# Rotation tables from tables held in pairs, ahead of slab 1's statistics, and slab 0's second token half in quarters

## The chip, the cores and the metric

The kernel runs on one NeuronCore of a Trainium2 chip. The core has five engines that run side by side, each with an instruction queue of its own that is worked off in order: TensorE (PE, matrix products), VectorE (DVE), ScalarE (ACT), GpSimd (POOL) and SyncE (SP, which here only issues DMAs). They meet through semaphores. TensorE writes to PSUM, which this kernel uses as eight banks of 128 x 512 fp32. The metric is device time in microseconds for one execution; all times below are microseconds unless marked otherwise.

## The reference

The input `x` has 2048 tokens of 512 features. What is computed, cut to what matters:

```python
xn = (x - mean(x)) / sqrt(var(x) + 1e-5)                 # per token
dt = exp(log_dt); Lam_bar = exp(dt * (Lambda_re + 1j * Lambda_im))
B_bar = ((Lam_bar - 1) / Lam)[:, None] * Bmat            # 512 complex states
Bu = einsum("bld,pd->blp", xn, B_bar)
for t in range(2048):
    h = Lam_bar * h + Bu[t]
s = 2 * einsum("blp,dp->bld", h, Cmat).real + xn * Dskip
g = silu((gelu(xn @ w_gate) * (xn @ w_up)) @ w_down)     # 512 -> 1376 -> 512
out = x + s * g
```

## The kernel before

**Tiling.** The tokens go in four slabs (`NS`) of 512 (`TS`), each in four blocks of 128 tokens. For a slab, `ffn` (L459) runs eleven steps `j` over the 1376 hidden features: gate and up products into two PSUM banks (`gu_mm`, L236), GELU and copy on ScalarE, their product on VectorE in pairs of steps (`at`). `u_pair` (L372) makes the products with B in two halves, `chain` rotates them by a complex table, runs the scans on VectorE and rotates back into `hst`. `down` (L482) multiplies `at` with `w_down` into `f_ps`, 11 products for each block. `y_mm` (L502) and `epi` (L514) of a slab run inside the `ffn` steps of the next one, at the steps that `Y_AT` names; `y_seed` (L497) fills their PSUM bank first, on ScalarE.

**Rotation.** The complex recurrence becomes a real one by rotating with cos and sin of the angle times the token number. The tables `cos_b` and `sin_b` hold 512 columns for each of four groups of states. They come from small ones: with token = 32a + b, cos and sin of 32a (`NA` = 16 values) and of b (`NB` = 32 values) are taken with ScalarE's Sin (`sh`, `ch`, 49 columns), and VectorE makes the large table with four products and two sums (L614, L624 to L628). The angles come from GpSimd, L206 to L214, out of `pf` (L205). GpSimd copies the values of 32a out to full width, `sa` and `ca` (L284, L285), so that the products read them densely.

**Order.** Every engine's order is the order of the program's text (`manual_schedule`). For VectorE a small planner writes it: `later` puts work in a list with a due time and a cost; `dve` gives out an operation that is due at a time, and ahead of it `drain` pops from the front of the list what fits by the clock `clk["dve"]`; `flush` pops up to a named item. The clock of TensorE advances by 0.2157 a product.

**Head of slab 0.** Ten filler products (`dummies`) surround the transpose of the small parameters. Blocks 0 and 1 are loaded first, their statistics (`bn`, `bn_end`), square root and reciprocal (`rstd0`) and norm (`norm0`) follow, TensorE transposes (`t_xn0`) and VectorE and ScalarE copy to `xnT`. `gu_mm` then runs the first 256 tokens of steps 0 to 3 (`SPLIT` = 4, `early`) while blocks 2 and 3 are prepared; one PSUM bank holds the transposes of both. `ffn` adds the second 256 tokens.

**Slab 1's input.** VectorE takes its statistics (L612), GpSimd its `rs`, VectorE norms it with `norm1` (L619), and SyncE issues four DMA transposes to `xnT` (`xn_out`, L585). These are issued in steps 3 to 6 of slab 0. At step 6 SyncE is also given four DMA transposes of C's real part, the two loads of `wd`, and four transposes of C's imaginary part (L651 to L658), in this order:

```python
                if 3 <= j < 3 + M:
                    flush(("xn", j - 3))
                    xn_out(1, j - 3, xs1[j - 3])
                if j == 2 + M:
                    load_c(0)
```

Ahead of them its queue holds the loads of tokens, gate and up weights and the transposes of B. `wd` is first read by slab 0's `down`, behind both `u_pair`s of slab 1, which read slab 1's `xnT`.

## Time and profile before

| | |
|---|---|
| median of 13 runs | 185.78 (185.56 to 186.16) |
| profiled execution, its own time | 186.08 |
| its span on the core | 183.5 |
| busy in the span: TensorE, VectorE, ScalarE, GpSimd | 176.1, 160.5, 116.9, 27.2 |
| slab 0's first product of step 4 starts | 15.88 |
| slab 1's `u_ps` products, slab 0's `f_ps` products start | 34.88, 41.78 |
| largest gap of TensorE behind the head | 1.17, at 101.86 |

The span runs from the first to the last instruction of the core; what the device time has beyond it, 2.6 here, lies around it. Starts are counted from the span's start. A row of the timeline gives start, length, engine, line of the kernel, operation, output and inputs, shapes, count, and in brackets how long the engine stood idle before it and what it waited for. Rows with DMA and an engine's name with q (SPq) are issues of transfers, whose length is that of the issue, not of the transfer. Lengths of products on TensorE overlap their neighbours.

### The profile page before, as it was taken

How to read it: one execution, taken by the hardware profiler on the slowest of the kernel's cores; microseconds unless marked ns; L12 is line 12 of the kernel's file. 1: busy time of each engine (PE TensorE's matmuls, PEld its weight loads, DVE VectorE, ACT ScalarE, POOL GpSimd, SP SyncE). 2: the span in 40 equal slices, each digit the busy share in tenths (PEclk: the TensorE clock that was granted, in tenths of full speed). 3: DMA queues.
4: the chain of work that ended last, by engine and by line, in shares of the span. 5: the costliest groups of instructions: out<-in, count | busy, mean ns of one | idle time of the engine just before them, and what ended most of it. 6: DMA issues, size and time to landing. Idle time of an engine off the chain costs nothing.

```text
span 183.5 us, 2441 instructions
## 1 busy us (share of the span) xinstructions
PE 176.1 (96%) x855; PEld 83.8 (46%) x855; DVE 160.5 (87%) x251; ACT 116.9 (64%) x207; POOL 27.2 (15%) x50
## 2 busy tenths in 40 slices
PE   6989999999999999999999799999999999999992
PEld 2666444544444444444444344444444444444451
DVE  3589999899999899899958999999999999996063
ACT  3299666668789974475499775667529445574510
POOL 3879917000700000000004000000000000000000
PEclk9999999999999999999999999999999999999999
DMA  5999594690001400101300023300000000000012
GB/s 159 299 350 158 101 238 108 186 278 0 0 0 29 84 5 29 50 7 30 113 4 0 0 59 84 88 5 0 0 0 0 0 30 32 29 29 0 0 47 68
DMA packets 25643, 12.37 MB, mean 67 GB/s; under 512 B 15808, under 2 KB 25632, under 8 KB 25632
## 3 DMA queue, kind: packets, MB, share of 16 engines
q1 hardware_dynamic: 25456, 12.16, 27.1%
q8 instruction: 6, 0.10, 0.2%
q10 hardware_dynamic: 176, 0.07, 0.1%
q14 instruction: 5, 0.04, 0.1%
HBM read 6.46 MB, written 2.10 MB: 47 GB/s over the span
## 4 chain that ended last, share of the span: by engine, by line
PE 73%; DVE 9%; ACT 8%; DMA 3%; POOL 2%; issue 2%; ACTq 1%; SPq 0%; DVEq 0%; POOLq 0%
PE up_ps L243 17%; PE g_ps L243 17%; PE f_ps L487 14%; PE y_ps L507 13%; PE u_ps L382 11%; DVE Ft L429 3%; ACT junk L552 2%; DMA x_tok<-in_A_x_dram 2%; DVE yg L520 2%; DVE pp L399 1%; DMA pv<-in_A_Dskip_dram 1%; ACT gt L471 1%; ACT ub L472 1%; ACT g L492 1%; DVE ot L521 1%
## 5 line engine op out<-in xcount | busy, mean ns | idle before, releaser
L243 PE MATMUL up_ps<-xnT,wu 128*128 128x512 bf16 (+2 forms) x192 | 45.7, 361 | 0.8 <-ACT xnT L201 0.8
L243 PE MATMUL g_ps<-xnT,wg 128*128 128x512 bf16 (+3 forms) x196 | 45.9, 357 | 0.3 <-DVE xnT L203 0.3
L487 PE MATMUL f_ps<-wd,at 128*128 128x512 bf16 (+1 forms) x176 | 38.9, 379 | 0.1
L471 ACT ACTIVATE gt<-g_ps 128x512 bf16<-128x512 f32 (+1 forms) x44 | 26.7, 608 | 17.0 <-PE g_ps L243 16.6
L472 ACT ACTIVATE ub<-up_ps 128x512 bf16<-128x512 f32 (+1 forms) x44 | 26.9, 612 | 6.7 <-PE up_ps L243 6.3
L429 DVE TENSOR_TENSOR_SCAN Ft<-rho,it,Wt 128x512 bf16<-128x512 f32 x24 | 29.3, 1267 | 0.0
L507 PE MATMUL y_ps<-C,hst 128*128 128x512 bf16 x120 | 28.0, 379 | 1.2 <-ACT y_ps L499 1.2
L382 PE MATMUL u_ps<-xnT,BT 128*128 128x512 bf16 x128 | 28.4, 379 | 0.0
L243 PEld LDWEIGHTS <-wu 128*128 128x128 bf16 (+1 forms) x192 | 19.2, 100 | 19.8 <-issue 1.0
L243 PEld LDWEIGHTS <-wg 128*128 128x128 bf16 (+1 forms) x196 | 19.3, 100 | 19.2 <-issue 0.4
L487 PEld LDWEIGHTS <-at 128*128 128x128 bf16 (+1 forms) x176 | 17.1, 98 | 21.1 <-DVE at L478 0.5
L387 ACT ACTIVATE U<-u_ps 128x512 bf16<-128x512 f32 x32 | 19.0, 597 | 9.8 <-PE u_ps L382 9.7
L382 PEld LDWEIGHTS <-BT 128*128 128x128 bf16 x128 | 12.5, 98 | 15.1
L492 ACT ACTIVATE g<-f_ps 128x512 f32<-128x512 f32 x16 | 9.5, 593 | 15.2 <-PE f_ps L487 15.2
L507 PEld LDWEIGHTS <-hst 128*128 128x128 bf16 x120 | 11.7, 98 | 15.5 <-issue 1.5
L520 DVE TENSOR_TENSOR yg<-y_ps,g 128x512 bf16<-128x512 f32 x15 | 10.2, 683 | 9.1 <-PE y_ps L507 9.0
L480 DVE TENSOR_TENSOR at<-gt,ub 128x1024 bf16<-128x1024 bf16 x20 | 13.6, 682 | 1.6 <-ACT ub L472 1.5
L403 DVE TENSOR_TENSOR hst<-pp,qq 128x1024 bf16<-128x1024 bf16 x16 | 10.4, 688 | 0.3
L403 DVE TENSOR_TENSOR Wt<-pp,qq 128x1024 bf16<-128x1024 bf16 x16 | 10.4, 686 | 0.2
L399 DVE TENSOR_TENSOR pp<-U,cos_b 128x2048 bf16<-128x2048 bf16 x8 | 9.7, 1219 | 0.0
L399 DVE TENSOR_TENSOR pp<-Ft,cos_b 128x2048 bf16<-128x2048 bf16 x8 | 9.7, 1217 | 0.0
L399 DVE TENSOR_TENSOR qq<-U,sin_b 128x2048 bf16<-128x2048 bf16 x8 | 9.7, 1216 | 0.0
(108 smaller groups left out, 153.6 us busy)
## 6 DMA issues: line engine op xcount, KB each, us to landing
out_dram<-ot SPq DMA_DIRECT2D x15, 128.0 KB, 1.7
x_tok<-in_A_x_dram SPq DMA_DIRECT2D x3, 512.0 KB, 6.8
wd<-in_B_w_down_dram SPq DMA_DIRECT2D x1, 1280.0 KB
wg<-in_B_w_gate_dram SPq DMA_DIRECT2D x2, 256.0 KB, 4.2
wu<-in_B_w_up_dram SPq DMA_DIRECT2D x2, 256.0 KB
wg<-in_B_w_gate_dram SPq DMA_DIRECT2D x1, 512.0 KB, 6.1
wu<-in_B_w_up_dram SPq DMA_DIRECT2D x1, 512.0 KB
wg<-in_B_w_gate_dram SPq DMA_DIRECT2D x1, 352.0 KB
```

The lines of the kernel that those rows point to most:

```text
L243: nc.tensor.matmul(ps[:fs, a:b], lhsT=w[:, kt, fsl], rhs=xnT[:, kt, s * TS + a : s * TS + b], start=(kt == 0), stop=(kt == KT - 1),)
L382: nc.tensor.matmul(u_ps[:, :], lhsT=BT[:, ri, kt, pt * P : (pt + 1) * P], rhs=xnT[:, kt, cols], start=(kt == 0), stop=(kt == KT - 1),)
L387: ACT(out=U[:, ri, q, :], in_=u_ps[:, :], func=AF.Copy)
L399: TT(out=box[key][:], in0=src()[:], in1=tab[:, hs, :].unsqueeze(1).to_broadcast(W), op=ALU.mult)
L403: return lambda: TT(out=dst()[i], in0=box["pp"][:, i, :, :], in1=box["qq"][:, 1 - i, :, :], op=op)
L429: nc.vector.tensor_tensor_scan(out=box["F"][:, ri, q, :], data0=rho[:, pt : pt + 1].to_broadcast([P, TS]), data1=box["W"][:, ri, q, :], in ...
L471: ACT(out=gt[:fs, i, :], in_=g_ps[:fs, :], func=AF.Gelu_apprx_tanh)
L472: ACT(out=ub[:fs, i, :], in_=u_ps[:fs, :], func=AF.Copy)
L480: dve(now() + lag, 0.63, lambda: TT(out=at[:, j - 1 : j + 1, :], in0=gt[:], in1=ub[:], op=ALU.mult))
L487: nc.tensor.matmul(f_ps[:, :], lhsT=at[:fs, k, m0 : m0 + P], rhs=wd[:fs, k, :], start=(k == 0), stop=(k == NFT - 1))
L507: nc.tensor.matmul(y_ps[:, :], lhsT=hst[:, j // NPT, j % NPT, m0 : m0 + P], rhs=C2[:, j // NPT, j % NPT, :], start=False, stop=(j == 2 * N ...
L520: TT(out=yg[:], in0=y_ps[:, :], in1=g2[:], op=ALU.mult)
```

## The change

Small tables in pairs: GpSimd no longer copies 32a's cos and sin to full width. It writes each value twice, side by side (`s2a`, `c2a`, 128 columns), and the four products read them with a five-dimensional pattern whose innermost dimension is the pair.

Order: the table's six operations stand at the front of VectorE's list. Slab 1's statistics follow them, popped at step 5, its `rs` behind them, the norms and the four transposes at step 6, and C and `wd` are issued at step 7. The products of slab 0's tokens with `Dskip` (`skip`) come behind the statistics.

Head: statistics, square root and reciprocal of blocks 0 and 1 come ahead of `pf` in the text; eight filler products and one instead of six and four; `Abs` moves behind the first Sin. `SPLIT` is 3; blocks 2 and 3 are transposed into a bank each, both copied by VectorE, and steps 0 (gate, up) and 1 (gate) take the second token half in quarters of 128, block 2 first. Step 3 runs whole.

Slab 2: slab 1's output products move from steps 3 to 6 to steps 4 to 7. The planner's starting clocks change with all this.

```diff
-    dummies(6)
+    dummies(8)
     pt_ps = psum.tile([P, 16], BF16, name="pt_ps", tag="ps")
     nc.tensor.transpose(pt_ps[:, :], pv[:, :], ident[0:16, 0:16])
-    dummies(4)
+    dummies(1)
...
+    for m in range(2):
+        bn(0, m)
+    bn_end(0, 0)
+    bn_end(0, 1)
+    rstd0(0, 2)
     ACT(out=pf[:], in_=pt_ps[:, :], func=AF.Copy)
...
-    for m in range(2):
-        bn(0, m)
-    bn_end(0, 0)
-    bn_end(0, 1)
-    rstd0(0, 2)
     xs = [norm0(0), norm0(1)]
...
-    ACT(out=kr[:], in_=ang[:], func=AF.Abs)
     rstd0(2, 4)
     ACT(out=tiny[:], in_=halfpi[:], func=AF.Sin)
     xs += [norm0(2), norm0(3)]
-    SPLIT = 4
+    SPLIT = 3
...
-    for up in range(2):
-        early[2, up] = gu_mm(0, 2, up, 0, TS // 2)
-    tp2 = psum.tile([P, 2, KT, P], BF16, name="tp", tag="ps")
-    for i in range(2):
-        t_xn0(2 + i, xs[2 + i], tp2[:, i, :, :])
-    for up in range(2):
-        early[3, up] = gu_mm(0, 3, up, 0, TS // 2)
-    xnT_out(nc.vector, 2, tp2[:, 0, :, :])
+    early[2, 0] = gu_mm(0, 2, 0, 0, TS // 2)
+    tps.append(t_xn0(2, xs[2]))
+    early[2, 1] = gu_mm(0, 2, 1, 0, TS // 2)
+    tps.append(t_xn0(3, xs[3]))
+    for m in range(2, M):
+        xnT_out(nc.vector, m, tps[m])
+    for m in range(2, M):
+        for j, up in ((0, 0), (0, 1), (1, 0)):
+            gu_mm(0, j, up, m * P, (m + 1) * P, early[j, up])
     ACT(out=sh[:], in_=ang[:], func=AF.Sin, scale=TWO_PI)
+    ACT(out=kr[:], in_=ang[:], func=AF.Abs)
     ACT(out=ch[:], in_=kr[:], func=AF.Sin, scale=-TWO_PI, bias=halfpi[:])
-    xnT_out(nc.scalar, 3, tp2[:, 1, :, :])
...
-    nc.gpsimd.tensor_copy(out=v4(sa[:]), in_=sh[:, :, NB : NB + NA].unsqueeze(3).to_broadcast(W4))
-    nc.gpsimd.tensor_copy(out=v4(ca[:]), in_=ch[:, :, NB : NB + NA].unsqueeze(3).to_broadcast(W4))
-    cB = ch[:, :, 0:NB].unsqueeze(2).to_broadcast(W4)
-    sB = sh[:, :, 0:NB].unsqueeze(2).to_broadcast(W4)
+    c2a, s2a = (consts.tile([P, NPT, NA, 2], BF16, name=n) for n in ("c2a", "s2a"))
+    for o, i in ((s2a, sh), (c2a, ch)):
+        nc.gpsimd.tensor_copy(out=o[:], in_=i[:, :, NB : NB + NA].unsqueeze(3).to_broadcast([P, NPT, NA, 2]))
+    sa, ca = (o[:].unsqueeze(3).to_broadcast(W5) for o in (s2a, c2a))
+
+    def of_b(t):
+        return t[:, :, 0:NB].rearrange("p k (b c) -> p k b c", c=2).unsqueeze(2).to_broadcast(W5)
+
+    cB, sB = of_b(ch), of_b(sh)
...
-    Y_AT = {1: (8, 9, 10, 11), 2: (3, 4, 5, 6), 3: (2, 4, 6, 8)}
+    Y_AT = {1: (8, 9, 10, 11), 2: (4, 5, 6, 7), 3: (2, 4, 6, 8)}
...
         if s == 0 and j < SPLIT:
-            g_ps, u_ps = (gu_mm(s, j, up, TS // 2, TS, early[j, up]) for up in range(2))
+            g_ps, u_ps = early[j, 0], early[j, 1]
+            for up in range(2):
+                if j == 2 or (j == 1 and up):
+                    gu_mm(s, j, up, TS // 2, TS, early[j, up])
...
-    clk["pe"] = 6.8
-    clk["dve"] = 13.1
-    clk["act"] = 12.4
+    clk["pe"] = 6.9
+    clk["dve"] = 10.6
+    clk["act"] = 12.6
...
-    ln_vector(1)
-    ln_vector_small(1)
-    later(13.0, 1.25, lambda: TT(out=v4(t2_[:]), in0=v4(sa[:]), in1=sB, op=ALU.mult))
+    later(10.5, 1.25, lambda: TT(out=v5(t2_[:]), in0=sa, in1=sB, op=ALU.mult))
+    later(11.2, 1.25, lambda: TT(out=v5(t1_[:]), in0=ca, in1=cB, op=ALU.mult))
+    later(11.2, 1.25, lambda: TT(out=cos_b[:], in0=t1_[:], in1=t2_[:], op=ALU.subtract))
+    later(11.2, 1.25, lambda: TT(out=v5(t1_[:]), in0=sa, in1=cB, op=ALU.mult))
+    later(11.2, 1.25, lambda: TT(out=v5(t2_[:]), in0=ca, in1=sB, op=ALU.mult))
+    later(11.2, 1.25, lambda: TT(out=sin_b[:], in0=t1_[:], in1=t2_[:], op=ALU.add))
+    for m in range(M):
+        later(0.0, 0.72, lambda m=m: (bn(1, m), bn_end(1, m)), "n1")
...
-    for m in range(M):
-        later(15.8, 0.36, lambda m=m: norm1(m), ("xn", m))
...
-                if 3 <= j < 3 + M:
-                    flush(("xn", j - 3))
-                    xn_out(1, j - 3, xs1[j - 3])
-                if j == 2 + M:
+                if j == 5:
+                    flush("n1")
+                    ln_vector_small(1)
+                    rs1_at = clk["dve"] + 2.4
+                if j == 6:
+                    for m in range(M):
+                        dve(max(rs1_at, now() - 0.8), 0.36, lambda m=m: norm1(m), 0.4)
+                        xn_out(1, m, xs1[m])
+                if j == 7:
                     load_c(0)
```

## The prediction

> **What bounds the kernel now.** I read the page's busy line first, then the timeline of TensorE for its gaps, then the queues that feed the first slab: SyncE, VectorE, the DMA packets.

> ```profile
> PE 176.1 (96%) x855; PEld 83.8 (46%) x855; DVE 160.5 (87%) x251; ACT 116.9 (64%) x207; POOL 27.2 (15%) x50
> ```

> TensorE is busy 96%, so the time is its work plus its gaps. Its timeline has few, and these rows carry them:

> ```profile
> 11.96 0.60 PE L243 MATMUL up_ps<-xnT,wu 128*128 128x256 bf16 x4 [0.79 <-ACT xnT L201]
> ...
> 34.88 7.07 PE L382 MATMUL u_ps<-xnT,BT 128*128 128x512 bf16 x32
> 41.78 9.68 PE L487 MATMUL f_ps<-wd,at 128*128 128x512 bf16 x44
> ...
> 101.86 1.89 PE L507 MATMUL y_ps<-C,hst 128*128 128x512 bf16 x8 [1.17 <-ACT y_ps L499]
> ```

> From 11.96 to the end only one gap is shown, 1.17 at 101.86. So a gain at the head counts in full unless a feeder becomes late, and a feeder that becomes late by more than its slack costs in full. The SyncE queue is the feeder that the change moves:

> ```profile
> 21.80 0.50 SPq L98 DMA_DIRECT2D wu<-in_B_w_up_dram  x1
> 22.42 5.13 SPq L587 DMA_TRANSPOSE xnT<-xn  x4
> 27.61 5.22 SPq L106 DMA_TRANSPOSE CT<-in_A_C_re_dram  x4
> 32.88 0.58 SPq L653 DMA_DIRECT2D wd<-in_B_w_down_dram  x1
> 33.50 0.65 SPq L657 DMA_DIRECT2D wd<-in_B_w_down_dram  x1
> ```

> It runs without a pause: the normalised slab 1 has been ready since about 20 (last L171 row of VectorE below), so nothing waits for data. `wd` goes out last, and its second piece lands 6.2 later, at 39.7; TensorE wants `wd` at 41.78.

> ```profile
> wd<-in_B_w_down_dram SPq DMA_DIRECT2D x1, 96.0 KB, 6.2
> ```

> The packets of 38.75 to 39.00 and of the next quarter microsecond show the last of `wd` (its rows are 1 KB; the transposes' packets are under 512 B):

> ```profile
> DMA packets 250, 0.07 MB, mean 275 GB/s; under 512 B 240, under 2 KB 250, under 8 KB 250
> DMA packets 171, 0.04 MB, mean 161 GB/s; under 512 B 171, under 2 KB 171, under 8 KB 171
> ```

> So the big piece of `wd` lands between 38.9 and 39.7; I take 39.4, a slack of 2.4 that no wait row shows. Last, VectorE around the tables:

> ```profile
> 11.11 2.46 DVE L160 BATCH_NORM_STATS2 st<-x_tok 128x6 f32<-128x512 bf16 x4
> 13.77 2.20 DVE L614 TENSOR_TENSOR t__264<-sa,sh 128x2048 bf16<-128x2048 bf16 x1
> ...
> 19.41 0.40 DVE L171 TENSOR_SCALAR xn<-x_tok,mv,rs 128x512 bf16<-128x512 bf16 x1
> ...
> 20.78 1.25 DVE L624 TENSOR_TENSOR t__263<-ca,ch 128x2048 bf16<-128x2048 bf16 x1
> ```

> Slab 1's statistics come first, the five other table operations (1.25 each) last. That is what the change turns round.

> [...] A transpose that waits for its source therefore holds every later DMA of SyncE. The trace agrees: output stores stood 101.3 in all on that queue for VectorE's `ot`, and the load of slab 3's tokens left only behind one of them, at 86.01. [...] the 2.20 product overlaps the wide GpSimd copy (12.97 to 14.86), the others take 1.25. [...] the trace shows full speed behind its 1.17 gap and nothing of longer ones.

> **The change part by part.** *Head.* Moving the square root ahead of `pf` starts it at about 4.36 (statistics end 4.30) instead of 4.58; eight dummies end at about 4.6 (start spacing 0.43), one more at 5.1, so slab 0's transposes start when their weights can load, about 5.55, not 6.08. First product at 6.7 (7.22 before), the second quarter after ACT's copy at 7.3 (about 7.6). Then four halves at 0.435: 9.26 with `[2,g]`. `Abs` no longer stands before the second square root: it starts at 8.1 (9.03), the norms end at 9.35 (10.27). `pf` is 0.3 later, so are GpSimd's angles (9.04), still before `sh` at 9.8. Transposes, `[2,u]`, transposes end at 10.23 (0.27 per four, from eight in 0.54). VectorE copies both blocks, to 10.14 and 10.84. Six quarters at 0.22 to 0.27 run 10.23 to 11.85, the rest of j=1, 2 (3 x 0.435) to 13.15, j=3 whole (1.73) to 14.9. Before, j=4 starts at 15.88. **Gain 1.0** (0.5 to 1.3; the clock of the first products varies). ACT's first GELU moves from 13.51 to about 12.4, so the PSUM banks free in time.

> *Tables.* Two GpSimd copies of 1.89 become 128-element copies (0.2 to 0.5, between the 49- and 196-element rows), hidden beside the slab's head. GpSimd's twelve coefficient operations then run at 11 to 17 instead of 18 to 23.5, ahead of `rs`; those that overlapped table operations before left these at 1.25, so I add nothing. The four products: low bound 1.2 each (as now, and never 2.20)[...]. I take 1.2[...].

> *VectorE's new order.* Following the planner's clocks (start 10.6) through `drain`: t2, t1, cos, t1 | at j1 | t2 | at j3 | sin | at j5 | statistics x4 (flushed at j=5) | z x4 | pp | norm x4. `pp` gets ahead of the norms because 24.31+1.17 is within 25.27+0.4. With durations of the trace: start 10.9; four table operations of about 1.23 to 15.85; at 0.6, t2 1.2, at 0.6, sin 1.2, at 0.6 to 20.05 (all three GELU pairs are ready before); statistics 4 x 0.80 (rows at 42.48 to 45.69) to 23.25; z 4 x 0.335 to 24.6; pp 1.15 to 25.75; first norm done 26.15. GpSimd's `rs` takes 2.2 after the last statistics (45.77 to 47.98 in slab 2), so 25.45: hidden by z and pp.

> *SyncE.* Its first transpose of slab 1 leaves at 26.2 instead of 22.42: **the queue is 3.8 late**, idle since 22.3. Queued behind it: three transposes, four of C (re), `wd`, `wd`'s end, four of C (im). First, xnT: last issue 30.05, landing 2.4 to 3.4 later, 33.5 at most; TensorE wants it at 33.9. It holds, by 0.4. Second, `wd`: 39.4 + 3.8 = 43.2; TensorE, 1.0 early, wants it at 40.8 and **stands 2.4**. Third, C (im): first block about 42.5; ACT wants it at 46.3, after `f_ps`.

> *Sum at `f_ps`.* It starts at 43.2 instead of 41.78: **+1.4**. The head's gain is wholly eaten: once `wd` ends last, only the queue's lateness less the slack counts (3.8 - 2.4). Behind it VectorE, some 2 earlier relative to TensorE than before, only waits longer for ACT's `tA`, and slabs 1 to 3 keep their distances to TensorE. [...] I add nothing for the clock.

> *Slab 2.* The first y product moves behind j=4. ACT does GELU and copy of j=3 (0.97) and one norm (0.71) ahead of the seed, so it ends at 103.4 and not 101.8; TensorE arrives at 102.4 and not 100.7. The gap is 1.05 instead of 1.17: **-0.1**. Bounds: 0 to -0.5 if a norm slips behind.

> Total +1.3: span 184.8, and with the 2.6 around it (186.08 less 183.5) 187.4 for an execution like the profiled one. That one lies 0.3 above the median 185.78, so I name **187.1**.

> **Rivals.** *A, the load is covered after all.* Place: `wd` before the first `f_ps`. Price: the head's 1.0 and slab 2's 0.1 then count, 184.7. It decides if the queue is under 2.4 late (break-even), in full under 1.4, that is with the first norm done by 24.8 or 23.8; or if the transfer lands in less than its 6.2. For it: 6.2 includes a queue behind C's packets till 33.9, and 1.4 MB at the 380 GB/s shown in the middle need only 3.7. Against: the same transposes precede it afterwards, and all but four VectorE durations are read from rows. *B, pairs read slowly.* [...] *C, it cancels*: slack 3 and lateness 3.1 leave +0.1 less 0.1, 185.8. Before, the big piece landing at 38.9 gives 2.9 of slack, so this is near one end of the bounds.

> **How the numbers follow.** My forecast 63%, B 15%, A 15%, C 7%. The forecast's own range is 186.2 to 188.3: slack 1.5 (landing 40.3, if 6.2 counts from the issue's end) to 2.9, queue late 3.3 to 4.4 (start of the tables 10.6 to 11.5). I give 184.9 to 189.6: it leaves out the deeper half of A and the upper half of B and its overshoot. A measurement of this kernel tells about 0.2% (0.37) from no change. Faster, from A: 15%; same, from C: 7%; slower, forecast and B: 78%.

> **What would show it.** Right: SyncE's transposes of xnT at about 26.2, not 22.4; `wd` issued near 36.7; a gap of about 2.4 before L487's first matmul, put down to a DMA of `wd`; j=4 on TensorE near 14.9; table products at 1.2; the gap before slab 2's first y product about 1. Wrong: L487 starting before 41.7[...]; or a gap at `u_ps` of slab 1 that is longer than the one at `f_ps`.

## The result, and the profile after

The kernel after takes **188.75 us** in the median of 11 runs (187.04 to 190.47), beside 185.87 for the kernel before (48 runs). The ratio is 1.0122, 95% interval 1.0099 to 1.0146: slower by about 1.2%. The forecast was 187.1, range 184.9 to 189.6. The ratio is taken without executions more than 1.5% above the fastest, so it lies below the quotient of the medians.

The executions differ, and their mean granted clock of TensorE says how. With the profiled one there are twelve:

| mean granted clock | executions | time | span |
|---|---|---|---|
| 1.0 | 4 | 187.04, 187.10, 187.15, 188.26 | 184.8 to 185.1 |
| 0.990 to 0.991 | 6 | 188.55 to 190.47 | 186.3 to 187.0 |
| 0.982 | 2 | 190.29, 190.61 | 188.0, 188.3 |

The profiled execution is the slowest, 190.61 with a span of 188.3. From the page, the busy line and the clock (40 slices of 4.7 us; each digit is tenths of full speed, 9 for 0.9 and more):

```profile
PE 178.1 (95%) x858; PEld 83.9 (45%) x858; DVE 160.6 (85%) x252; ACT 116.5 (62%) x206; POOL 23.2 (12%) x50
...
PEclk9789999997899999999999999999999999999999
```

TensorE's clock was at half speed twice, from 7.29 to 10.70 and from 44.83 to 48.25, each time for 3.41. The timeline of TensorE shows what this cost:

```profile
7.04 1.93 PE L242 MATMUL g_ps<-xnT,wg 128*128 128x128 bf16 x12 [0.19 <-DVE xnT L203]
8.77 1.91 PE L242 MATMUL up_ps<-xnT,wu 128*128 128x256 bf16 x8
...
16.30 1.03 PE L242 MATMUL g_ps<-xnT,wg 128*128 128x512 bf16 x4
...
35.30 7.07 PE L386 MATMUL u_ps<-xnT,BT 128*128 128x512 bf16 x32
...
45.22 11.15 PE L494 MATMUL f_ps<-wd,at 128*128 128x512 bf16 x44 [2.85 <-DMA wd<-in_B_w_down_dram]
...
108.39 1.89 PE L514 MATMUL y_ps<-C,hst 128*128 128x512 bf16 x8 [1.07 <-ACT y_ps L506]
```

Ahead of `f_ps` TensorE stands 2.85, waiting for a load of `wd`; before, it did not stand there at all. Then the same 44 products take 11.15, where before they took 9.68. In stretches of this execution (start and end, length, busy time and count of TensorE, clock, share and rate in GB/s of the DMA engines):

```profile
40.00:42.00 2.00, 2.00 (x11) 1.00 0.96 309
42.00:44.00 2.00, 0.37 (x2) 1.00 1.14 361
44.00:46.00 2.00, 0.78 (x2) 0.71 1.48 80
46.00:48.00 2.00, 2.00 (x6) 0.50 0.87 169
48.00:50.00 2.00, 2.00 (x10) 0.94 0.00 0
```

The clock drops to half while TensorE stands and comes back a little over 48: in 46 to 48 six products start where eleven did before the stand. SyncE's queue shows why `wd` came late (issues only):

```profile
22.31 0.50 SPq L98 DMA_DIRECT2D wu<-in_B_w_up_dram  x1
27.58 5.12 SPq L594 DMA_TRANSPOSE xnT<-xn  x4
32.75 5.17 SPq L106 DMA_TRANSPOSE CT<-in_A_C_re_dram  x4
37.97 0.58 SPq L662 DMA_DIRECT2D wd<-in_B_w_down_dram  x1
38.60 0.65 SPq L666 DMA_DIRECT2D wd<-in_B_w_down_dram  x1
```

The queue is idle from 22.8 to 27.6, waiting for slab 1's norms, and `wd` leaves at 37.97 where it left at 32.88 before. VectorE's rows ahead of that:

```profile
12.45 1.25 DVE L619 TENSOR_TENSOR t__276<-s2a,sh 128x2048 bf16<-128x2048 bf16 x1
...
26.01 1.22 DVE L403 TENSOR_TENSOR pp<-U,cos_b 128x2048 bf16<-128x2048 bf16 x1
27.15 1.37 DVE L171 TENSOR_SCALAR xn<-x_tok,mv,rs 128x512 bf16<-128x512 bf16 x4
```

The first table product takes 1.25 with the pairs. The norms stand last, behind the six table operations, the statistics, the products with `Dskip` and `pp`.

The sum for this execution: `f_ps` starts 3.44 later (45.22 less 41.78); its products take 1.47 longer; the gap at slab 2 is 0.10 shorter (1.07 for 1.17). Together 4.81, and the span is 4.8 longer.

### The profile page after: what moved, and what is told of

It is laid out like the page before. It is cut to its first block, busy times and chain, and to the rows that moved or that the text cites. A ratio compares the mean times of both kernels' runs of the same rounds, so it can differ in the third digit from the quotient of the medians.

```text
span 188.3 us, 2448 instructions
## 1 busy us (share of the span) xinstructions
PE 178.1 (95%) x858; PEld 83.9 (45%) x858; DVE 160.6 (85%) x252; ACT 116.5 (62%) x206; POOL 23.2 (12%) x50
## 4 chain that ended last, share of the span: by engine, by line
PE 58%; DVE 23%; DMA 7%; ACT 4%; SPq 4%; issue 2%; DVEq 0%; ACTq 0%
PE f_ps L494 15%; PE up_ps L242 13%; PE g_ps L242 13%; PE y_ps L514 13%; DMA wd<-in_B_w_down_dram 4%; PE u_ps L386 4%; DMA x_tok<-in_A_x_dram 4%; DVE Ft L433 3%; SPq L106 3%; DVE pp L403 2%; ACT junk L559 2%; DVE qq L403 2%; DVE st L160 2%; DVE at L487 2%; DVE yg L527 1%
## 5 line engine op out<-in xcount | busy, mean ns | idle before, releaser
L242 PE MATMUL g_ps<-xnT,wg 128*128 128x512 bf16 (+3 forms) x200 | 46.6, 358 | 0.3 <-DVE xnT L203 0.2
L242 PE MATMUL up_ps<-xnT,wu 128*128 128x512 bf16 (+3 forms) x192 | 46.6, 367 | 0.0
L494 PE MATMUL f_ps<-wd,at 128*128 128x512 bf16 (+1 forms) x176 | 40.3, 389 | 2.9 <-DMA wd<-in_B_w_down_dram 2.9
L499 ACT ACTIVATE g<-f_ps 128x512 f32<-128x512 f32 x16 | 9.5, 593 | 19.7 <-PE f_ps L494 19.7
L487 DVE TENSOR_TENSOR at<-gt,ub 128x1024 bf16<-128x1024 bf16 x20 | 13.6, 680 | 0.9 <-ACT ub L479 0.9
L160 DVE BATCH_NORM_STATS2 st<-x_tok 128x6 f32<-128x512 bf16 x12 | 8.0, 673 | 2.3 <-DMA x_tok<-in_A_x_dram 2.3
```

The source lines that it names most:

```text
L242: nc.tensor.matmul(ps[:fs, a:b], lhsT=w[:, kt, fsl], rhs=xnT[:, kt, s * TS + a : s * TS + b], start=(kt == 0), stop=(kt == KT - 1),)
L487: dve(now() + lag, 0.63, lambda: TT(out=at[:, j - 1 : j + 1, :], in0=gt[:], in1=ub[:], op=ALU.mult))
L494: nc.tensor.matmul(f_ps[:, :], lhsT=at[:fs, k, m0 : m0 + P], rhs=wd[:fs, k, :], start=(k == 0), stop=(k == NFT - 1))
```

## The experiments

Each starts from the kernel after, unless said otherwise. The theory is that of the prediction: the head gains, the late `wd` takes more than it gave. The ratios are to the kernel before on the same chip (185.88 to 185.97). Starts named below are those of the experiment's profiled execution.

### wd ahead of everything that waits (e1_wd_early)

```diff
     load_gu(3)
+    nc.sync.dma_start(out=wd[:, 0 : NFT - 1, :], in_=...)
+    nc.sync.dma_start(out=wd[:FL, NFT - 1, :], in_=B_w_down[(NFT - 1) * P : F, :])
...
                 if j == 7:
                     load_c(0)
-                    (the same two loads)
                     load_c(1)
```

> The changed kernel with one edit: both loads of wd are issued right behind the last gate and up weights, ahead of the wait for slab 1's norms. Theory of the late load: the stand of 2.85 before the first f_ps product is gone, f_ps starts at about 41 to 42, and the time falls by 2.3 or more below the changed kernel, to 184.7 where TensorE keeps its clock in the head and to 186.4 where it loses one window there. Rival, the head is what costs and the load only hides it: f_ps still starts at 43 or later and the time stays within 0.5 of the changed kernel.

Measured: 184.54 (184.02 to 186.09, 18 runs), ratio 0.9930 (0.9911 to 0.9950). `wd` is issued at 22.54; `f_ps` starts at 40.51 without a stand. The granted clock is at least 0.996 in all 18. So the order of one queue turns the change from 1.2% slower to 0.7% faster.

### The old order of VectorE and SyncE (e5_old_order)

Everything else of the change stays: head, pairs, quarters, slab 2's steps.

```diff
-    clk["dve"] = 10.6
+    clk["dve"] = 13.1
...
-    later(10.5, 1.25, ...)            # table operations first, "n1" behind
+    ln_vector(1)
+    ln_vector_small(1)
+    later(13.0, 1.25, ...)            # one product; then skip, norm1, the other five
...
-                if j == 5:            # flush("n1"); norms and transposes at 6, C and wd at 7
+                if 3 <= j < 3 + M:
+                    flush(("xn", j - 3))
+                    xn_out(1, j - 3, xs1[j - 3])
+                if j == 2 + M:
```

> The changed kernel with the order of before for VectorE and SyncE: slab 1's statistics and norms ahead of the table, its transposes in steps 3 to 6, C and wd at step 6; head, pairs, quarters and slab 2's steps stay as changed. Theory of the late load: SyncE runs without a pause again, wd is issued near 32.9, f_ps starts at about 40.6 without a stand, time 184.4 to 184.8, equal to the version with wd early. Rival, the table ahead of the statistics carries part of the gain: clearly above 184.8.

Measured: 184.53 (184.08 to 185.52, 6 runs), ratio 0.9932 (0.9908 to 0.9957). SyncE's queue of this kernel is the old one again:

```profile
21.88 0.51 SPq L98 DMA_DIRECT2D wu<-in_B_w_up_dram  x1
22.50 5.12 SPq L594 DMA_TRANSPOSE xnT<-xn  x4
27.68 5.16 SPq L106 DMA_TRANSPOSE CT<-in_A_C_re_dram  x4
32.88 0.58 SPq L660 DMA_DIRECT2D wd<-in_B_w_down_dram  x1
```

`f_ps` starts at 40.11, no stand. The same time as e1 by another way: it is the lateness of `wd`, and not where VectorE makes its tables, that costs.

### wd ahead of C only (e8_wd_before_c)

```diff
                 if j == 7:
+                    (the two loads of wd)
                     load_c(0)
-                    (the two loads of wd)
                     load_c(1)
```

> The changed kernel with wd issued behind slab 1's four transposes but ahead of the four of C's real part: 5.2 earlier than in the changed kernel, still 3.6 behind the norms. Theory of the late load: wd lands at about 38 to 39, ahead of 40.6, so no stand: 184.4 to 184.8, as with wd ahead of the norms. Rival, wd's transfer and the transposes hinder each other: f_ps waits for wd or u_ps for xnT, above 185.

Measured: 184.54 (184.21 to 185.18, 6 runs), ratio 0.9928 (0.9905 to 0.9950). The queue still starts its transposes late, at 25.92, but `wd` leaves at 31.10 and `f_ps` starts at 40.24 without a stand. In the kernel before, `wd` stood behind the same four transposes of C without harm; with the norms late as well, their 5.2 of issue makes the loss. The late norms alone do no harm.

### The same lateness in the kernel before (e4_before_wd_late)

```diff
 (the kernel before)
                     load_c(0)
+                    load_c(1)
                     (the two loads of wd)
-                    load_c(1)
```

> The kernel before with one edit: the two loads of wd stand behind the four transposes of C's imaginary part, 5.4 later in SyncE's queue; nothing else moves. Theory of the late load: lateness less slack, 5.4 less 2.4, so f_ps starts at about 44.8 and the time is 3.0 more than before, 188.8, with 1.7 more where the clock drops behind the stand. If the slack were 4 or more, as rival A of the prediction needs, it is 187.2 or less.

Measured: 189.70 (188.50 to 193.28, 6 runs), ratio 1.0188 (1.0138 to 1.0238). Its `wd` is issued at 37.73. TensorE's timeline in the profiled execution, one of the three at 188.50 to 188.66:

```profile
35.01 7.07 PE L382 MATMUL u_ps<-xnT,BT 128*128 128x512 bf16 x32
44.57 9.67 PE L487 MATMUL f_ps<-wd,at 128*128 128x512 bf16 x44 [2.49 <-DMA wd<-in_B_w_down_dram]
```

Here the products behind a stand of 2.49 ran at full pace. The other three executions, 190.73 to 193.28, had a mean clock of 0.990 to 0.991 and spans 2.3 to 3.0 longer. The stand comes with the late load, without any of the change; and the clock falls in three of the six executions only.

### More work in the stand (e7_stand_filled)

Ten more filler products, whose results nothing reads, between slab 1's `u_ps` and slab 0's `f_ps`.

```diff
+            if s == 0:
+                dummies(10)
             for m in range(M):
                 g2s[s, m] = down(s, m, ats[s])
```

> The changed kernel with ten filler products (2.2 of TensorE's time) between slab 1's u_ps and slab 0's f_ps, where TensorE stands for 2.4 to 2.9; their result is not used. wd stays late. Theory that the stand lowers TensorE's clock: f_ps starts at the same time, the clock stays at 1.00 behind it, and the executions at 188.5 and above become rare: median 187.0 to 187.3, so more work and less time. Rival, the clock drops by chance: the spread of 187.0 to 190.5 and the median of 188.7 stay, or rise by up to 2.2 where the filler delays f_ps.

Measured: 187.43 (187.24 to 188.47, 6 runs), ratio 1.0087 (1.0063 to 1.0112), clock 0.998 or more in all six. The timeline of TensorE:

```profile
33.83 7.07 PE L386 MATMUL u_ps<-xnT,BT 128*128 128x512 bf16 x31
40.73 2.32 PE L153 MATMUL w_ps<-warm 128*128 128x512 bf16 x10
43.87 9.67 PE L494 MATMUL f_ps<-wd,at 128*128 128x512 bf16 x43 [0.81 <-DMA wd<-in_B_w_down_dram]
```

`wd` is issued at 36.79 and `f_ps` starts at 43.87, no earlier than in e2 below (43.12), and the median is still 1.3 below that of the kernel after. The mean clock fell in none of six executions, in the kernel after in 8 of 12. The intervals of the two ratios overlap (to 1.0112 here, from 1.0099 there), so the count of falls carries the reading more than the times do: it is the idle time, and not the late load as such, that takes the clock down.

### The filler products of the head (e2_fillers, e3_both, e10_before_fillers)

e2 is the kernel after with the 6 and 4 fillers of before; e3 has these and the early `wd` of e1; e10 is the kernel before with the 8 and 1 of after.

```diff
-    dummies(8)
+    dummies(6)
...
-    dummies(1)
+    dummies(4)
```

> The changed kernel with the filler products of before, six and four instead of eight and one; wd stays late. Theory of the late load and the clock: the half-speed stretch of TensorE near 7.5 to 10.5 is gone in nearly all executions, the stand before f_ps stays at 2 to 3, the clock behind the stand can still drop; time 187.0 to 188.7, with the executions above 190 gone. Rival, the half-speed stretch in the head is chance and not the fillers: the spread of 187.0 to 190.5 stays as it is.

> Both edits: wd early and fillers six and four. Theory of the late load and the clock: no stand before f_ps and full clock throughout, 184.5 to 185.0, so faster than the kernel before by 0.8 to 1.2. Rival, the head gives nothing: 185.8 as before.

> The kernel before with only the number of filler products in the head changed, to the 8 and 1 of the kernel after. Theory (before's head is bound by the chain of the angles and tables, so fewer fillers open a gap and nothing moves): 185.8 to 186.2, no change against before. Rival (the fillers alone carry the head's gain, as the 0.85 between e1 and e3 could suggest): about 185.0, ratio 0.995.

Measured:

| | median (range, runs) | ratio to before |
|---|---|---|
| e2 | 188.17 (187.02 to 190.66, 6) | 1.0090 (1.0059 to 1.0120) |
| e3 | 185.39 (184.28 to 187.44, 22) | 0.9952 (0.9932 to 0.9971) |
| e10 | 186.43 (185.96 to 187.06, 22) | 1.0025 (1.0012 to 1.0038) |

In e2 `f_ps` starts behind a stand with `wd` issued at 36.38:

```profile
43.12 9.67 PE L494 MATMUL f_ps<-wd,at 128*128 128x512 bf16 x44 [2.62 <-DVE st L160]
```

The row names `st` of VectorE as what ended last. The large load of `wd` carries no landing time in this trace; the start 6.74 behind its issue, beside 6.84 to 7.25 in the kernel after, e4 and e7, is why the wait is put down to `wd` here. The median lies in the range that was expected, but one execution took 190.66 at a mean clock of 0.990, so the spread of the kernel after stayed, as the rival had it.

e3 lies above the 184.5 to 185.0 that were expected. Against e1 it makes 8 and 1 worth about 0.85 where the head counts. In the kernel before they gain nothing, they lose 0.55, which neither theory had: its executions lie at 185.96 to 186.33 and at 186.53 to 187.06, and the profiled one, of the second group, has its first products at a slower pace:

```profile
8.95 1.79 PE L243 MATMUL up_ps<-xnT,wu 128*128 128x256 bf16 x8
10.58 0.60 PE L243 MATMUL g_ps<-xnT,wg 128*128 128x256 bf16 x4
```

The eight take 402 ns each; the next four take 272, as the same shapes do in the kernel before. The mean clock says 1.0 in both. But the views count the time ahead of the clock's first record as full speed. In the kernel before the records begin at 6.56, and the fillers, all ahead of it, take 606 to 634 ns; in the kernel after they begin at 3.88, and the fillers wholly ahead of it take 607 to 631 and the one behind it 380, as long as an `f_ps` product at full clock (379). The eight products above take 418 each in the stretch of half clock of the kernel after. The estimate from these lengths is that the slow pace in e10 is half clock too, from the start of the program to near 10.5. Why it lasts longer here is not settled. What follows is only that the count of fillers isn't by itself the gain; it pays with the rest of the new head.

### The pairs alone (e6_before_pairs)

The kernel before with the small tables in pairs and the five-dimensional products, nothing else.

```diff
-    nc.gpsimd.tensor_copy(out=v4(sa[:]), in_=sh[:, :, NB : NB + NA].unsqueeze(3).to_broadcast(W4))
-    nc.gpsimd.tensor_copy(out=v4(ca[:]), in_=ch[:, :, NB : NB + NA].unsqueeze(3).to_broadcast(W4))
+    for o, i in ((s2a, sh), (c2a, ch)):
+        nc.gpsimd.tensor_copy(out=o[:], in_=i[:, :, NB : NB + NA].unsqueeze(3).to_broadcast([P, NPT, NA, 2]))
```

> The kernel before with the pairs alone: two copies of 128 columns instead of 2048 on GpSimd, the products read pairs; order and head as before. Theory: the first table product takes 1.25 instead of 2.20 and GpSimd is 3.2 less busy, but neither is on the chain that ends last: same time as before, 185.6 to 186.0. Rival, VectorE's 0.95 counts: 185.0 or less.

Measured: 185.95 (185.65 to 187.34, 14 runs), ratio 1.0001 (0.9983 to 1.0019). VectorE's timeline:

```profile
13.88 1.23 DVE L617 TENSOR_TENSOR t__262<-s2a,sh 128x2048 bf16<-128x2048 bf16 x1
15.03 1.09 DVE L580 TENSOR_TENSOR x_tok<-xn,Db 128x512 bf16<-128x512 bf16 x3
```

The first product takes 1.23 instead of 2.20, a second of VectorE's time saved, and the kernel is no faster: VectorE had room there.

### The gap at slab 2 (e9_load_x3_early)

e8, with slab 3's tokens loaded ahead of slab 0's last output store instead of behind it.

```diff
+            if s == 1:
+                load_x(3)
             if s > 0 and NFT in Y_AT[s]:
                 epi(s - 1, M - 1, ...)
-            if s == 1:
-                load_x(3)
```

> The kernel of e8 (wd ahead of C re) with one more move: slab 3's token load is issued ahead of slab 0's last output store instead of behind it, about 5 us earlier on SyncE. Theory (the gap of 1.07 ahead of slab 2's first y product is ScalarE running late because its pass over slab 3's tokens waits about 2.6 for that load): the wait goes, ScalarE's later work and the seed of y come earlier, the gap goes, and the time is about 183.4, 1.0 to 1.1 below e8's 184.54. Rival (the gap is ScalarE's own order of work, the load is not what is late): 184.5, no change against e8.

Measured: **183.40** (182.96 to 183.57, 6 runs), ratio 0.9856 (0.9834 to 0.9879). Its slowest execution is faster than e8's fastest (184.21). ScalarE's timeline around the statistics of slab 3, in e8:

```profile
85.13 0.60 ACT L499 ACTIVATE g<-f_ps 128x512 f32<-128x512 f32 x1 [2.21 <-PE f_ps L494]
88.42 0.63 ACT L559 ACTIVATE junk<-x_tok 128x512 bf16<-128x512 bf16 x1 [2.69 <-DMA x_tok<-in_A_x_dram]
```

and in e9, where the load is issued at 79.06 instead of 84.47:

```profile
85.50 0.60 ACT L499 ACTIVATE g<-f_ps 128x512 f32<-128x512 f32 x1 [2.21 <-PE f_ps L494]
85.99 0.62 ACT L559 ACTIVATE junk<-x_tok 128x512 bf16<-128x512 bf16 x1
```

TensorE's first y product of slab 2, in e8 and then in e9:

```profile
101.99 1.89 PE L514 MATMUL y_ps<-C,hst 128*128 128x512 bf16 x8 [1.12 <-ACT y_ps L506]
```

```profile
101.38 1.89 PE L514 MATMUL y_ps<-C,hst 128*128 128x512 bf16 x8 [0.15 <-ACT y_ps L506]
```

Most of the gap was ScalarE held up by a load, and the load by a store that waited in front of it. ScalarE waits for the same load in the kernels before and after (2.67 and 2.63), where the edit itself was not tried. This version beats both kernels.

## Why the prediction was right, and where it was not

**The direction and its cause stand.** "The queue is 3.8 late" and "stands 2.4" are what the profiles show: where the head wasn't disturbed the first transpose of xnT left at 25.92 to 26.41 (26.2 forecast), `wd` at 36.38 to 36.79 (36.7), and `f_ps` started at 43.12 in e2 (43.2). The three executions at 187.04 to 187.15 agree with the forecast of 187.1. e1, e5 and e8 show that nothing but the lateness of `wd` takes the gain; e4 makes the same kind of loss in the kernel before. That a waiting DMA holds back those behind it is in the traces: the wait of SyncE's queue from 22.8 to 27.6 held `wd` back to 37.97, and slab 3's load left at 84.47 behind a waiting store in e8 and at 79.06 ahead of it in e9.

**The step that failed** is the end of *Sum at `f_ps`*: "I add nothing for the clock." The longest gap behind the head that the trace of before shows is 1.17, so what a stand of 2.4 does to the clock was not shown. In 8 of 12 executions the mean clock was down, six by 0.009 to 0.010 and two by 0.018. Read from the spans, that is 1.5 to 2.2 for one such loss (186.3 to 187.0 less 184.8) and 3.2 to 3.5 for two; one stretch at half speed of the 3.41 that the profiled execution shows would cost 1.7, by an estimate from that length, and did cost 1.47 there, where TensorE stands in 0.4 of it. In e4 the three executions with a fall are 2.3 to 3.0 longer, more than one such stretch by that estimate; the rest is open. In the kernel after, the falls move the median from 187.1 to 188.75. Where the clock fell is seen in the profiled execution alone; that the stand is the cause in the others too rests on e7, whose six executions lost nothing. The profiled execution shows half clock behind a stand of 2.85, those of e4 and e2 show full pace behind 2.49 and 2.62 (9.67 for the 44 products in both); what sets them apart is not shown.

**The range** of 184.9 to 189.6 holds 188.75, and that is luck. Its upper part was room for a later queue and for rival B; what filled it was the clock. The prediction's own forecast, 186.2 to 188.3, doesn't hold it; worked out from the ends of slack and lateness that it names (1.5 to 2.9, 3.3 to 4.4), that range would be 186.1 to 188.6.

**The slack** of `wd`, 2.4 forecast, was 1.7 to 2.2. `f_ps` started 6.74 (e2), 6.84 (e4), 7.08 (e7) and 7.25 (after) behind the issue of `wd`, and in the kernel before TensorE wanted it 8.90 behind (41.78 less 32.88). The landing time was read too early by 0.2 to 0.7. In e2 the queue, 0.3 earlier than forecast, made up for it, so the 43.12 is partly two small errors that cancel. The other slack, 0.4 for slab 1's `xnT`, was as thin as it was read: in e1 `u_ps` waits 0.19 for it.

**Head.** A gain of 1.0 was forecast, step 4's products at 14.9. In the five profiled executions with this head and full clock in it (e1, e5, e7, e8, e9) they start at 14.21 to 14.84: 1.0 to 1.7, so the forecast is their low end. The first product starts at 6.36 in e8 (6.7 forecast), and the quarters take 1.3 from 9.96 on (1.6 from 10.23). With the queue mended the kernel gains 1.4 (185.94 less 184.54 in e8). In the profiled execution of after, the head itself lost a stretch to half speed (the 1.93 and 1.91 above; the same groups take 1.31 and 1.04 in e8), which made VectorE and the queue later by another 1.4 and `f_ps` with them. In the 36 executions of e1, e5, e8 and e9, with the same head, the mean clock never fell below 0.996; in one of the 22 of e10, without any stand at `f_ps`, it fell to 0.991, at a place that is not on record. What sets off the loss in the head is open.

**Tables** were right: the four products take 1.25 to 1.28 in the kernel after and 1.23 to 1.26 in e6, so rival B, slow reads of pairs, falls; no trace had shown them. GpSimd's copies take 0.29 each in the kernel after (1.89 before), and no product took 2.20 in either.

**Slab 2**: 1.05 forecast, 1.07 found. The step named ScalarE's order as the cause of the length; what e9 shows is that most of it was a load waiting behind a store. So the number came out right on an incomplete cause.

**Rivals.** A, "the load is covered after all", with 184.7, is what e8 measures (184.54) once the transposes of C stand behind `wd`; in the kernel as it was changed its condition, a queue less than 2.4 late, didn't hold. C, the tie, asked for slack 3 and didn't come.

## What to carry to other kernels

A load that depends on nothing goes ahead of every DMA of its queue that waits for an engine; when such a wait is moved later, list what is queued behind it and when each is wanted; here the order alone was worth 4.2 (188.75 less 184.54 in e1). A stand on TensorE of 2.5 to 2.9 us, as here, is priced with its own length and with a possible stretch of half clock behind it, which cost 1.47 in the profiled execution and 1.5 to 2.2 by the spans of six others. Once the bound engine has a single gap left, follow its chain back to the issue of the transfer: 1.0 of the 1.1 at slab 2 was two lines of order.

## What the runs showed of the hardware that was not expected

In the profiled execution of the kernel after, TensorE's clock fell to half, for 3.41, within a stand of 2.85. The mean clock was at 0.991 or less in 8 of 12 executions of the kernel after (stand of 2.85 in the profiled one), 3 of 6 of e4 (2.49) and 1 of 6 of e2 (2.62); in the 100 executions of e1, e3 and e5 to e10, which have no stand or a filled one, it was so once, in e10. Ten filler products of 2.3 in all in the stand kept it up (0.998 or more in the six executions of e7), and the median was 1.3 lower, although they compute nothing.

A small operand read as pairs, each pair sixteen times over, costs VectorE about as much as a dense one: 1.23 to 1.28 for 2048 bf16 columns in the kernel after and e6, beside 1.25 to 1.28 for dense operands in the kernel before where GpSimd didn't copy.

The first products of a kernel can run at a slower pace (402 ns for 272) with a mean clock of 1.0, as in e10: in the kernels before and after the records of the clock begin only at 6.56 and 3.88, and fillers that take 606 ns or more ahead of that count as full speed.
